# A transformer block on one core: first MLP cut into blocks of 464 tokens instead of 384, with fewer resident weight slots

## The chip, the cores and the metric

The kernel runs on one core of a Trainium2 chip. Its engines work side by side, each through its own list of instructions: TensorE (PE) multiplies matrices, VectorE (DVE), ScalarE (ACT) and GpSimd (POOL) work element by element, and SyncE (SP) issues the DMAs. The metric is the device time of one launch in microseconds; three runs of the kernel before gave 1130.8, 1130.98 and 1131.02, with a median of 1130.98.

## The reference

```
scores = (q @ k^T) / 8 + bias(pos)            # 4 batches, 8 heads, 576 positions, 64 per head
attn   = softmax(scores) @ v                  # -> x: 2304 tokens x 512
h = x @ w_in;   g = h - tanh(h)               # first MLP:  512 -> 2048
x = g @ w_out                                 #             2048 -> 512
gate = sigmoid(x @ w_gate);  val = x @ w_val  # second MLP: 512 -> 1536, twice
out  = (gate * val) @ w_out2                  #             1536 -> 512
```

The bias is a small MLP of the relative position. All is fp32; the MLP weights come in as float64.

## The kernel before

There are three stages: bias and attention, the first MLP, the second MLP. Each fp32 operand of an MLP product is split into a high part that PE multiplies at full rate (`fp32r`) and the rest, and a product is three matmuls, high by high, low by high, high by low (`P3`, L694, L764).

**First MLP.** The 2304 tokens are cut into blocks of `TBS[1]` = 384 columns, six of them. A step `n` of `STEPS` takes one block and two of the sixteen slices of 128 hidden units. It goes through the engines as a pipeline: `first` (PE, 24 matmuls into one of two PSUM tiles, `even` and `odd`), `second` (ACT, squares and tanh), `third` (DVE, five operations on both slices at once, which replace h - tanh(h) by a polynomial where h is small), `fourth` (ACT and POOL, split into high and low), `fifth` (PE, 24 matmuls into four accumulators `acc`), and at the end of a half-block `sixth` (the accumulators go to `o` and by DMA to `x2s`). PE takes `first(n)` and then `fifth(n-2)`. Half of the hidden units are done for all blocks, then the other half, whose `sixth` adds (L780) to what the first half stored. PSUM's eight banks are full: twice two for `up`, four for `acc`.

**Weights.** `Weights` turns each float64 tile of 512 KB into fp32: `load` (DMA, two buffers `wraw`), `scan` (ACT), `make` (four DVE operations, L578 to L576), `split` (ACT high, POOL low). The first 32 items (`RES`) are the first MLP's; each keeps a slot of SBUF, 15 of them are made during the attention. The other 36 are the second MLP's: their tiles are stored in DRAM (`wsc`). `W.step` does one item at a step of the first MLP: in steps 2 to 47, but not in three of the last (`X0_STEPS`) nor where a `sixth` of the second half is due (four more steps), which makes 39. The rest is done in the second MLP by the generator `convert`, which is asked once in each product slot and has 7 stops for an item.

**Second MLP.** `PAIRS` lists 18 rounds, each with 128 times two hidden units of gate and value, over a third of the tokens. Seven products (a Strassen form, `PRODUCTS`) of six matmuls each are done for two halves (`m`), so a round has 14 product slots (`slot2`), with `down` (six 512-column matmuls, L922) in every odd one. A round reads nine weight tiles of 512 KB back from `wsc` (`feed`, L855), in strict order, into any slot that is free. There are 14 such slots: 12 of the first MLP's (`RING_SLOTS`) as its last block leaves them and two new ones.

The `tile` calls say what may be overwritten when; the order on each engine is the order of the code.

Of the kernel before, what the change touches and what calls it, by code (L numbers as in the profile page):

```python
# [19 lines left out]
NT = NB * S  # L20
# [7 lines left out]
def bias_phase(tc, pools, par, bsc, during):  # L28
# [9 lines left out]
    heat = yp.tile([128, 512], F32, name="heat", bufs=1)  # L38
    nc.gpsimd.memset(heat, 0.0)
    ph = spare.tile([128, 2, 512], F32, name="sc")  # L40
    for i in range(HEAT):
        T.matmul(ph[:, i % 2], heat[:, 0:128], heat, start=True, stop=True)
    scl = yp.tile([128, S // 4], F32, name="scl", bufs=1)
# [421 lines left out]
STEPS = [(1, b, f) for b in range(NT // TBS[1]) for f in range(HALF)]  # L465
STEPS += [(1, b, f) for b in range(NT // TBS[1]) for f in range(HALF, NF1 // NPR)]
# [7 lines left out]
X_SLOTS, T_SLOTS, RING_SLOTS = tuple(range(14)), (14, 15), 12  # L474
STAGE1 = (0, 1, 2, 3)
# [14 lines left out]
class Weights:  # L490


    def __init__(self, nc, wi, wo, wg, wv, wo2, stage, wsc):
        self.nc, self.stage, self.wsc = nc, stage, wsc
        col = lambda w, n, f, k0, nk: dram_ap(w.bitcast(I32), 256 * f + 256 * n * k0, [[2 * n, 128], [256 * n, nk], [1, 256]])
        row = lambda w, f: dram_ap(w.bitcast(I32), 128 * f * 2 * DM, [[2 * DM, 128], [1, 2 * DM]])
        self.of = {}
        use = [("i", f) for f in range(FA)] + [("o", f) for f in range(FA)]
        for f in range(FA, NF1):
            use += [("i", f), ("o", f)]  # L500
        self.items = []
# [12 lines left out]
        self.clock = self.lag = 0  # L514
        self.pending = []
# [73 lines left out]
    def split(self):  # L589
        i = self.done  # L590
        if i >= min(self.made, RES):
            return [], []
        self.done += 1
        w = self.out[i] = self.slot(i)
# [71 lines left out]
def mlps(tc, st, xr, x0, W, xs, x2s, y2s, out, consts):  # L666
# [5 lines left out]
    TB = TBS[1]  # L672
    xt, xraw = {}, {}

    def x_load(blk, kt):
        kind, b, half = blk
        m = xr.tile([128, TB], F32, name="xm")
        nc.sync.dma_start(m, xs[128 * kt:128 * kt + 128, TB * b:TB * b + TB])
        xraw[blk, kt] = m

    def x_split(blk, kt):
        m = xraw.pop((blk, kt))
        t = xh[BLOCKS.index(blk) % 2].tile([128, 2, TB], F32R, name="xt")
# [6 lines left out]
    def project(w, blk, p):  # L690
        for kt in range(4):
            x = xt[blk, kt]
            for i, (a, c) in enumerate(P3):
                T.matmul(p[:, 0:TB], w[:, a, 128 * kt:128 * kt + 128], x[:, c], start=(kt == 0 and i == 0), stop=(kt == 3 and i == 2))  # L694

    ph, s1, s2, ac, part = {}, {}, {}, {}, {}

    def first(n):
        kind, b, f = STEPS[n]
        p = (even, odd)[n % 2].tile([128, 2, 512], F32, name="up")  # L700
        ph[n] = p[:, :, 0:TB]
# [34 lines left out]
    def halves(x):  # L736
        h, l = (ps.tile([128, TB], F32R, name=y) for y in ("gh", "gl"))
# [14 lines left out]
    def fifth(n):  # L752
# [6 lines left out]
        for j in range(NPR):  # L759
            w = W.get("o", NPR * f + j)  # L760
            h, l = parts[j]
            for d in range(4):
                for i, (a, c) in enumerate(((0, h), (1, h), (0, l))):
                    T.matmul(ac[blk][d][:, 0:TB], w[:, a, 128 * d:128 * d + 128], c, start=(begin and j == 0 and i == 0),  # L764
                             stop=(end and j == NPR - 1 and i == 2))

    def partial(n):
        kind, b, f = STEPS[n]
        for d in range(4):
            o = ob.tile([128, DM], F32, name="o")  # L770
            nc.sync.dma_start(o[:, 0:TB], x2s[128 * d:128 * d + 128, TB * b:TB * b + TB])
            part[b, d] = o

    def sixth(n):
        kind, b, f = STEPS[n]
        blk = block(n)
        for d, p in enumerate(ac.pop(blk)):
            if blk[2] == 1:
                o = part.pop((b, d))
                V.tensor_add(o[:, 0:TB], p[:, 0:TB], o[:, 0:TB])  # L780
            else:
                o = ob.tile([128, DM], F32, name="o")
                (V.tensor_copy if d % 2 else A.copy)(o[:, 0:TB], p[:, 0:TB])  # L783
            W.later(lambda d=d, o=o: nc.sync.dma_start(x2s[128 * d:128 * d + 128, TB * b:TB * b + TB], o[:, 0:TB]))
# [25 lines left out]
    def src_load(tau, kt):  # L810
        sx[kt] = x0.tile([128, TP], F32, name="xt")
# [47 lines left out]
    freed = {W.of[k, f]: LAST[1, f // NPR] + (3 if k == "o" else 1) for k in "io" for f in range(FA, NF1)}  # L859
    RING = sorted(freed, key=lambda i: (freed[i], i))  # L860

    def convert():
        while W.made <= W.n:
            highs, lows, mixes, conv = W.step()
            for i, f in enumerate(conv[:2]):
                f()
                yield i == 0
# [8 lines left out]
            yield False  # L876
# [177 lines left out]
    for n in range(N1 + 3):  # L1054
        if n < N1:
            W.tick()
        if n == 2:
            acc = st.enter_context(tc.tile_pool(name="ps_a", bufs=4, space=PSUM, side="right"))
        acts = second(n - 1) if ok(n - 1) else []
# [3 lines left out]
        if 2 <= n < N1 and n not in X0_STEPS and not any(ends(m) and block(m)[2] for m in due(n - 1, 2)):  # L1063
# [15 lines left out]
        if n == N1:  # L1079
# [5 lines left out]
            W.open(st.enter_context(tc.tile_pool(name="wx", bufs=1)), RES, RES + 2)  # L1085
            free += [RES, RES + 1]
# [6 lines left out]
        for m in due(n - 1, 2):  # L1093
            if ends(m):
# [50 lines left out]
def tile_attention_then_two_mlps(ctx: ExitStack, tc: tile.TileContext, qT, kT, vP, par, wi, wo, wg, wv, wo2, ident, out, xs=None):  # L1145
# [8 lines left out]
    with tc.manual_schedule():  # L1154
# [49 lines left out]
        W.open(ctx.enter_context(tc.tile_pool(name="wb", bufs=1, side="right")), EARLY + MORE, RES)  # L1204
# [58 lines left out]
```

## Time and profile before

| | |
|---|---|
| median of three runs | 1130.98 us |
| profiled execution, its own time | 1131.97 us |
| its span | 1130.2 us |
| PE busy | 1113.5 us, 99% |
| DVE / ACT / POOL busy | 809.6 / 669.5 / 642.6 us |
| first MLP on PE | from 301.8 us to 719.4 us, mixed at both ends with its neighbours |

The profile is that of one execution; its own time is 1.0 us above the median of the timed runs, and 1.8 us of it lie outside the span. Busy times of PE are sums over matmuls whose ends are modelled and overlap, so the pace of PE is read from the starts of matmuls in the timeline, not from their durations.

### The profile page before, as it was taken

How to read it: one execution, taken by the hardware profiler on the slowest of the kernel's cores; microseconds unless marked ns; L12 is line 12 of the kernel's file. 1: busy time of each engine (PE TensorE's matmuls, PEld its weight loads, DVE VectorE, ACT ScalarE, POOL GpSimd, SP SyncE). 2: the span in 40 equal slices, each digit the busy share in tenths (PEclk: the TensorE clock that was granted, in tenths of full speed). 3: DMA queues.
4: the chain of work that ended last, by engine and by line, in shares of the span. 5: the costliest groups of instructions: out<-in, count | busy, mean ns of one | idle time of the engine just before them, and what ended most of it. 6: DMA issues, size and time to landing. Idle time of an engine off the chain costs nothing.

```text
span 1130.2 us, 20776 instructions
## 1 busy us (share of the span) xinstructions
PE 1113.5 (99%) x7324; PEld 982.6 (87%) x7324; DVE 809.6 (72%) x1444; ACT 669.5 (59%) x1320; POOL 642.6 (57%) x597
## 2 busy tenths in 40 slices
PE   8999999999999999999999999999999999999998
PEld 3466677777789999999999999999999999999997
DVE  8988888888589988898888888556566444434423
ACT  8987787887667767677667667235354332423221
POOL 0046767767555645596858666465486574524532
PEclk9999999999999999999999999999999999999999
DMA  7845455463223323366564665987987898667671
GB/s 255 287 151 174 139 163 165 144 193 112 83 76 105 124 85 109 120 205 201 204 214 159 229 200 215 345 323 273 341 329 283 321 380 306 238 238 268 234 271 57
DMA packets 107783, 235.14 MB, mean 208 GB/s; under 512 B 12704, under 2 KB 53152, under 8 KB 107680
## 3 DMA queue, kind: packets, MB, share of 16 engines
q1 hardware_dynamic: 107536, 233.69, 59.7%
q8 instruction: 58, 0.95, 0.3%
q14 instruction: 45, 0.37, 0.1%
q10 hardware_dynamic: 144, 0.13, 0.0%
HBM read 172.55 MB, written 61.22 MB: 207 GB/s over the span
## 4 chain that ended last, share of the span: by engine, by line
PE 88%; DVE 4%; POOL 2%; ACT 2%; issue 2%; DMA 2%; DVEq 0%; SPq 0%; POOLq 0%; ACTq 0%
PE sum L906 23%; PE acc L764 16%; PE up L694 16%; PE acc L922 9%; PE sc L243 6%; PE pt L285 5%; PE pv L343 5%; PE up L922 4%; DVE y L68 2%; PE pv L340 2%; PE bt L82 1%; DMA wsc<-w 1%; POOL n L275 1%; DVE n L257 1%; PE pf L290 1%
## 5 line engine op out<-in xcount | busy, mean ns | idle before, releaser
L906 PE MATMUL sum<-w,w 128*128 128x384 f32 x1512 | 279.8, 335 | 0.2 <-ACT e L970 0.2
L906 PEld LDWEIGHTS sum<-w,w 128*128 128x128 f32 x1512 | 265.5, 188 | 10.0 <-ACT e L970 0.6
L694 PE MATMUL up<-xt,w 128*128 128x384 f32 x1152 | 208.4, 335 | 0.3 <-DVE t L734 0.3
L694 PEld LDWEIGHTS up<-xt,w 128*128 128x128 f32 x1152 | 200.1, 188 | 2.2 <-issue 1.6
L764 PE MATMUL acc<-gh,w 128*128 128x384 f32 x768 | 195.4, 335 | 0.6 <-DVE o L780 0.5
L275 POOL TENSOR_SCALAR n<-n,rec 128x576 f32<-128x576 f32 x144 | 108.4, 766 | 131.6 <-DVE rec L271 128.8
L745 POOL TENSOR_TENSOR gl<-t,gh 128x384 fp32r<-128x384 f32 x96 | 103.8, 1102 | 89.3 <-issue 53.9
L585 POOL TENSOR_TENSOR w<-wu,w 128x512 fp32r<-128x512 f32 x86 | 125.9, 1476 | 25.0 <-ACT w L587 25.0
L764 PEld LDWEIGHTS acc<-gh,w 128*128 128x128 f32 x768 | 138.2, 188 | 1.9 <-DVE o L783 1.1
L962 POOL TENSOR_TENSOR gl<-e,gh 128x384 fp32r<-128x384 f32 x54 | 59.1, 1096 | 121.8 <-ACT gh L738 121.7
L764 PE MATMUL acc<-gl,w 128*128 128x384 f32 x384 | 128.3, 334 | 0.0
L257 DVE CUSTOM_DVE_ANT_0 n<-sc,bias 128x576 f32<-128x576 f32 x144 | 103.9, 755 | 20.9 <-PE sc L243 18.9
L264 ACT ACTIVATE n<-n,mn 128x576 f32<-128x576 f32 x144 | 111.8, 787 | 0.3 <-DVE mn L257 0.3
L725 ACT ACTIVATE z<-z,c 128x768 f32<-128x768 f32 x48 | 45.1, 941 | 77.0 <-DVE up L722 77.0
L922 PE MATMUL acc<-w,gh 128*128 128x512 f32 x288 | 89.5, 392 | 0.0
L738 ACT CAST gh<-t 128x384 fp32r<-128x384 f32 x114 | 57.7, 515 | 53.0 <-POOL t L998 51.5
L730 DVE TENSOR_TENSOR t<-up,t 128x768 f32<-128x768 f32 x48 | 45.9, 957 | 54.0 <-ACT t L711 53.4
L987 DVE TENSOR_TENSOR e<-sum,e 128x384 f32<-128x384 f32 x70 | 38.9, 556 | 62.8 <-PE sum L906 62.1
L285 PE MATMUL pt<-ident,n 128*128 128x128 f32 x576 | 80.1, 279 | 1.7 <-POOL n L275 1.2
L685 POOL TENSOR_TENSOR xt<-xm,xt 128x384 fp32r<-128x384 f32 x48 | 49.3, 1048 | 48.6 <-ACT xt L684 47.1
L285 PEld LDWEIGHTS pt<-ident,n 128*128 128x128 f32 x576 | 62.6, 140 | 13.4 <-issue 8.6
L343 PE MATMUL pv<-at,vs 128*64 128x320 f32 (+1 forms) x512 | 73.2, 409 | 0.0
(115 smaller groups left out, 2125.3 us busy)
## 6 DMA issues: line engine op xcount, KB each, us to landing
w<-wsc SPq DMA_DIRECT2D x162, 512.0 KB, 6.1
wsc<-w SPq DMA_DIRECT2D x54, 512.0 KB, 5.7
wraw<-in_wo SPq DMA_DIRECT2D x28, 512.0 KB, 4.2
xm<-xs SPq DMA_DIRECT2D x48, 192.0 KB, 3.2
x2s<-o SPq DMA_DIRECT2D x48, 192.0 KB, 3.9
wraw<-in_wi SPq DMA_DIRECT2D x16, 512.0 KB, 4.1
xt<-x2s SPq DMA_DIRECT2D x20, 384.0 KB, 8.0
wraw<-in_wg SPq DMA_DIRECT2D x24, 256.0 KB, 3.4
```

The lines of the kernel that those rows point to most:

```text
L243: T.matmul(sc[u, t][:, hf, 0:288], q[r, 128 * s:128 * s + 128], k[r, o:o + 288], start=(i == 0), stop=(i == 2))
L257: V.tensor_tensor_reduce(n.rearrange("p (a b) -> p a b", a=2), s[:, :, 0:288], bias[t].rearrange("p (a b) -> p a b", a=2), -0.125, 3.0e38, ...
L264: A.activation(n, n, AF.Exp, bias=m, scale=-1.0, accum_out=nsum[u, t // 4][:, t % 4:t % 4 + 1])
L275: G.tensor_scalar(n, n, nrec[u, t // 4][:, t % 4:t % 4 + 1], 1.0, ALU.mult, ALU.mult)
L285: T.transpose(pt[:, i], n[:, o:o + 128], ident)
L343: T.matmul(p[0][64 * a:64 * a + 64, 0:N], v[:, c - 1, a], main[:, c - 1, a * N:a * N + N], start=False, stop=(c == 4))
L585: self.nc.gpsimd.tensor_sub(w[:, 1], x, w[:, 0].bitcast(F32))
L694: T.matmul(p[:, 0:TB], w[:, a, 128 * kt:128 * kt + 128], x[:, c], start=(kt == 0 and i == 0), stop=(kt == 3 and i == 2))
L745: G.tensor_sub(l, x[:, j], h.bitcast(F32))
L764: T.matmul(ac[blk][d][:, 0:TB], w[:, a, 128 * d:128 * d + 128], c, start=(begin and j == 0 and i == 0), stop=(end and j == NPR - 1 and i = ...
L906: T.matmul(p, w[:, a, o:o + 128], x[:, c], start=(fresh and kp == 0 and i == 0), stop=(kp == 1 and i == 2), skip_group_check=True)
L922: T.matmul(sums[3 * t + d], x[:, c], w[:, a], start=(begin and i == 0), stop=(end and i == 2))
```

## The change

The first MLP's blocks are 464 tokens wide, with 448 in the last, so there are five; its tiles are allocated 512 columns wide (`TA`), and every use takes the columns that the block has. To make room, the 32 items of the first MLP share 28 slots: the items 28 to 31 go into the slots 0 to 3 (`HOME`) once the first half no longer needs these, and the order of the items is changed so that these are `w_in` tiles. In the second MLP 8 slots of the first MLP and 4 new ones take the reloads, 12 in all. `sixth` of the second half is moved to the front of its step, DVE does the five operations of `third` straight after it, and the step now converts a weight item as others do. `W.step` starts at step 3. `convert` has 5 stops for an item instead of 7, and a raw load is issued one slot after its buffer is free instead of two. In the bias stage two small tiles share memory with others.

```diff
-TBS = (None, 384, 384)
+TBS = (None, 512, 384)
+BW1 = 464
+BLK = [(BW1 * b, min(BW1, NT - BW1 * b)) for b in range(-(-NT // BW1))]
-RES = 32
+RES, NSLOT = 32, 28
+HOME = {28: 0, 29: 1, 30: 2, 31: 3}
-X_SLOTS, T_SLOTS, RING_SLOTS = tuple(range(14)), (14, 15), 12
-STAGE1 = (0, 1, 2, 3)
+X_SLOTS, T_SLOTS, RING_SLOTS, MORE2 = (10, 11, 12, 13, 4, 5, 6, 7, 8, 9, 0, 1, 2, 3), (14, 15), 8, 4
+STAGE1 = (6, 7, 8, 9)
...
-                T.matmul(p[:, 0:TB], w[:, a, 128 * kt:128 * kt + 128], x[:, c], start=(kt == 0 and i == 0), stop=(kt == 3 and i == 2))
+                T.matmul(p[:, 0:x.shape[-1]], w[:, a, 128 * kt:128 * kt + 128], x[:, c], start=(kt == 0 and i == 0), stop=(kt == 3 and i == 2))
...
-            self.later(self.load, 2)
+            self.later(self.load, 1)
...
             for i, f in enumerate(conv[:2]):
                 f()
-                yield i == 0
+                if i == 0:
+                    yield True
...
             for f in mixes:
                 f()
-            yield False
             W.scan()
             yield True
...
+        sums_in = [m for m in due(n - 1, 2) if ends(m) and block(m)[2]]
+        for m in sums_in:
+            sixth(m)
...
-        if 2 <= n < N1 and n not in X0_STEPS and not any(ends(m) and block(m)[2] for m in due(n - 1, 2)):
+        if 3 <= n < N1 and n not in X0_STEPS:
...
+        if sums_in:
+            zip_run(vecs)
+            vecs = []
         zip_run(vecs, conv)
...
-            W.open(st.enter_context(tc.tile_pool(name="wx", bufs=1)), RES, RES + 2)
-            free += [RES, RES + 1]
+            W.open(st.enter_context(tc.tile_pool(name="wx", bufs=1)), NSLOT, NSLOT + MORE2)
+            free += range(NSLOT, NSLOT + MORE2)
```

**PE, in the second half of the first MLP.** Before, a step's 24 matmuls of `first` and the start of `fifth`:

```order
L694 MATMUL up<-xt,w_2388 128x384 x12
L694 MATMUL up<-xt,w_2629 128x384 x12
L764 MATMUL acc<-gh,w_3355 128x384 x2
L764 MATMUL acc<-gl,w_3355 128x384
L764 MATMUL acc<-gh,w_3355 128x384 x2
```

And of the change:

```order
L699 MATMUL up<-xt,w_5585 128x464 x12
L699 MATMUL up<-xt,w_5777 128x464 x12
L769 MATMUL acc<-gh,w_6133 128x464 x2
L769 MATMUL acc<-gl,w_6133 128x464
L769 MATMUL acc<-gh,w_6133 128x464 x2
```

The pattern of a step is the same; a matmul has 464 columns instead of 384, and there are 40 such steps instead of 48, so 1920 matmuls (1536 of 464 columns and 384 of 448) instead of 2304.

**DVE, where a half-block of the second half ends** (`o<-acc,o` is `sixth`, the rows on `up` and `t` are `third`, those on `wu` are `make`). Before:

```order
L734 COPY_PREDICATED t<-z,up 128x768
L730 TENSOR_TENSOR t<-up,t 128x768
L731 SCALAR_TENSOR_TENSOR up<-z,up 128x2x384
L722 SCALAR_TENSOR_TENSOR up<-z,up 128x2x384
L733 SCALAR_TENSOR_TENSOR up<-q,up 128x2x384
L734 COPY_PREDICATED t<-z,up 128x768
L780 TENSOR_TENSOR o<-acc,o 128x384 x4
L730 TENSOR_TENSOR t<-up,t 128x768
L578 TENSOR_SCALAR wu<-wu 128x512
```

And of the change:

```order
L739 COPY_PREDICATED t<-z,up 128x2x464
L787 TENSOR_TENSOR o<-acc,o 128x464 x4
L735 TENSOR_TENSOR t<-up,t 128x2x464
L736 SCALAR_TENSOR_TENSOR up<-z,up 128x2x464
L727 SCALAR_TENSOR_TENSOR up<-z,up 128x2x464
L738 SCALAR_TENSOR_TENSOR up<-q,up 128x2x464
L739 COPY_PREDICATED t<-z,up 128x2x464
L582 TENSOR_SCALAR wu<-wu 128x512
L583 TENSOR_SCALAR wu<-wu 128x512
L584 SCALAR_TENSOR_TENSOR wu<-wraw,wu 128x512
L580 SCALAR_TENSOR_TENSOR wu<-wraw,wu 128x512
```

The four additions stand ahead of the step's five operations instead of behind them, and a weight item follows where there was none.

**SP, at the passage to the second MLP** (`w<-wsc` is a reload; the number after `wsc` is the tile's place in its round). Before:

```order
L784 DMA x2s<-o 128x384 x4
L855 DMA w_9146<-wsc_4_69 128x1024
L855 DMA w_9148<-wsc_5_70 128x1024
L855 DMA w_9150<-wsc_6_71 128x1024
L855 DMA w_9152<-wsc_7_72 128x1024
L855 DMA w_9197<-wsc_8_73 128x1024
L855 DMA w_9199<-wsc_0_74 128x1024
L771 DMA o<-x2s 128x384 x4
L855 DMA w_9251<-wsc_1_75 128x1024
L855 DMA w_9253<-wsc_2_76 128x1024
L855 DMA w_9255<-wsc_3_77 128x1024
L855 DMA w_9257<-wsc_4_78 128x1024
```

And of the change:

```order
L791 DMA x2s<-o 128x464 x4
L862 DMA w_8442<-wsc_4_69 128x1024
L862 DMA w_8444<-wsc_5_70 128x1024
L862 DMA w_8489<-wsc_6_71 128x1024
L862 DMA w_8491<-wsc_7_72 128x1024
L862 DMA w_8493<-wsc_8_73 128x1024
L862 DMA w_8495<-wsc_0_74 128x1024
L777 DMA o<-x2s 128x448 x4
L862 DMA w_8547<-wsc_1_75 128x1024
L862 DMA w_8549<-wsc_2_76 128x1024
```

The first loads are the same, but they end two tiles earlier: the place 2 of the second round instead of the place 4, because there are 12 slots instead of 14.

## Rows read from the trace of the kernel before

**Rows 1.** The page, part 1: busy time of the engines over the span.
```profile
PE 1113.5 (99%) x7324; PEld 982.6 (87%) x7324; DVE 809.6 (72%) x1444; ACT 669.5 (59%) x1320; POOL 642.6 (57%) x597
```

**Rows 2.** Stretches: PE, PEld, DVE, ACT, POOL busy; PEclk, DMA share, GB/s.
```profile
320.00:704.00 384.00, 383.13 (x2204) 381.54 (x2203) 336.49 (x429) 267.50 (x434) 252.59 (x209) 1.00 0.49 164
...
735.00:960.00 225.00, 225.00 (x1180) 209.53 (x1179) 123.04 (x199) 84.18 (x169) 135.60 (x116) 1.00 0.86 319
```

**Rows 3.** Timeline of PE in the first MLP: start, length, line, count.
```profile
669.97 4.32 PE L694 MATMUL up<-xt,w 128*128 128x384 f32 x24
674.13 0.51 PE L764 MATMUL acc<-gh,w 128*128 128x384 f32 x2
...
686.61 4.32 PE L694 MATMUL up<-xt,w 128*128 128x384 f32 x24
691.45 0.59 PE L764 MATMUL acc<-gh,w 128*128 128x384 f32 x2 [0.52 <-DVE o L780]
```

**Rows 4.** Timeline of PE in the kernel's last microseconds, 512 columns alone.
```profile
1120.01 0.61 PE L922 MATMUL acc<-w,gh 128*128 128x512 f32 x2
...
1124.77 0.61 PE L922 MATMUL acc<-w,gh 128*128 128x512 f32 x2
```

**Rows 5.** Timeline of PE in the second MLP, 384 and 512 columns by turns.
```profile
799.84 2.24 PE L906 MATMUL sum<-w,w 128*128 128x384 f32 x12
801.92 0.63 PE L922 MATMUL acc<-w,gh 128*128 128x512 f32 x2
...
803.31 2.25 PE L906 MATMUL sum<-w,w 128*128 128x384 f32 x12
```

**Rows 6.** Timeline of PE at the start of the first MLP.
```profile
299.97 0.66 PE L285 MATMUL pt<-ident,n 128*128 128x128 f32 x4
301.31 0.63 PE L285 MATMUL pt<-ident,n 128*128 128x128 f32 x4 [0.69 <-POOL n L275]
...
327.19 0.34 PE L764 MATMUL acc<-gl,w 128*128 128x384 f32 x1
327.81 4.46 PE L694 MATMUL up<-xt,w 128*128 128x384 f32 x24 [0.27 <-DVE t L734]
```

**Rows 7.** Timeline of POOL there.
```profile
294.95 1.99 POOL L685 TENSOR_TENSOR xt<-xm,xt 128x384 fp32r<-128x384 f32 x2
296.91 4.35 POOL L275 TENSOR_SCALAR n<-n,rec 128x576 f32<-128x576 f32 x6
```

**Rows 8.** Groups by line: count, busy, mean ns, idle before.
```profile
L722 DVE SCALAR_TENSOR_TENSOR up<-z,up 128x768 f32<-128x768 f32 x48 | 45.6, 951 | 0.2
L734 DVE COPY_PREDICATED t<-z,up 128x768 f32<-128x768 int32 x48 | 50.8, 1058 | 0.8
L578 DVE TENSOR_SCALAR wu<-wu 128x512 f32<-128x512 f32 x68 | 62.6, 921 | 0.3
L576 DVE SCALAR_TENSOR_TENSOR wu<-wraw,wu 128x512 int32<-128x512 int32 x68 | 56.7, 834 | 0.1
L579 DVE TENSOR_SCALAR wu<-wu 128x512 int32<-128x512 int32 x68 | 32.4, 476 | 0.0
L780 DVE TENSOR_TENSOR o<-acc,o 128x384 f32<-128x384 f32 x24 | 11.8, 551 | 2.0 <-PE acc L764 2.0
L939 DVE TENSOR_TENSOR o<-acc,o 128x512 f32<-128x512 f32 x7 | 4.8, 685 | 0.0
L685 POOL TENSOR_TENSOR xt<-xm,xt 128x384 fp32r<-128x384 f32 x48 | 49.3, 1048 | 48.6 <-ACT xt L684 47.1 <-DMA xm<-xs 1.3
L585 POOL TENSOR_TENSOR w<-wu,w 128x512 fp32r<-128x512 f32 x86 | 125.9, 1476 | 25.0 <-ACT w L587 25.0
```

**Rows 9.** DMA from 735 to 960 us: rate in 40 slices, the queue.
```profile
GB/s 295 208 330 381 386 226 387 405 202 155 397 415 371 224 294 396 272 169 396 413 145 162 290 405 410 410 385 411 326 99 312 400 402 414 350 373 409 124 240 379
...
q1 hardware_dynamic: 24014, 71.60, 85.4%
```

**Rows 10.** The reload's line L855: landing over the whole kernel.
```profile
DMA to landing us min/median/max: 3.1/6.1/10.3
```

More of the change, by code (lines that the diff above doesn't have):

```diff
@@ L37, in bias_phase @@
     w1c, b1c, wb, ps = pr[:, 0:1], pr[:, 1:2], pr[:, 4:36], pr[:, 36:36 + S // 4]
-    heat = yp.tile([128, 512], F32, name="heat", bufs=1)
+    heat = yp.tile([128, S], F32, name="y")
     nc.gpsimd.memset(heat, 0.0)
@@ L41, in bias_phase @@
     for i in range(HEAT):
-        T.matmul(ph[:, i % 2], heat[:, 0:128], heat, start=True, stop=True)
-    scl = yp.tile([128, S // 4], F32, name="scl", bufs=1)
+        T.matmul(ph[:, i % 2], heat[:, 0:128], heat[:, 0:512], start=True, stop=True)
+    scl = ps
     V.tensor_scalar(scl, ps, w1c, None, ALU.mult)
@@ L464 @@
 HALF = FA // NPR
-STEPS = [(1, b, f) for b in range(NT // TBS[1]) for f in range(HALF)]
-STEPS += [(1, b, f) for b in range(NT // TBS[1]) for f in range(HALF, NF1 // NPR)]
+STEPS = [(1, b, f) for b in range(len(BLK)) for f in range(HALF)]
+STEPS += [(1, b, f) for b in range(len(BLK)) for f in range(HALF, NF1 // NPR)]
 LAST = {(k, f): n for n, (k, b, f) in enumerate(STEPS)}
@@ L498, in __init__ @@
         use = [("i", f) for f in range(FA)] + [("o", f) for f in range(FA)]
-        for f in range(FA, NF1):
+        for f in range(FA, FA + 4):
             use += [("i", f), ("o", f)]
+        use += [("o", f) for f in range(FA + 4, NF1)] + [("i", f) for f in (14, 15, 12, 13)]
         self.items = []
@@ L593, in split @@
         self.done += 1
-        w = self.out[i] = self.slot(i)
+        w = self.out[i] = self.slot(HOME.get(i, i))
         def low():
@@ L671, in mlps @@
     nq, nz, warm = consts
-    TB = TBS[1]
+    TA, TB = TBS[1:]
     xt, xraw = {}, {}
@@ L676, in x_load @@
         kind, b, half = blk
-        m = xr.tile([128, TB], F32, name="xm")
-        nc.sync.dma_start(m, xs[128 * kt:128 * kt + 128, TB * b:TB * b + TB])
+        c0, w = BLK[b]
+        m = xr.tile([128, TA], F32, name="xm")[:, 0:w]
+        nc.sync.dma_start(m, xs[128 * kt:128 * kt + 128, c0:c0 + w])
         xraw[blk, kt] = m
@@ L682, in x_split @@
         m = xraw.pop((blk, kt))
-        t = xh[BLOCKS.index(blk) % 2].tile([128, 2, TB], F32R, name="xt")
+        t = xh[BLOCKS.index(blk) % 2].tile([128, 2, TA], F32R, name="xt")[:, :, 0:BLK[blk[1]][1]]
         A.copy(t[:, 0], m)
@@ L708, in second @@
         p = ph[n]
-        t, z, q = (k.tile([128, 2, TB], F32, name=x) for k, x in ((pk, "t"), (pm, "z"), (pq, "q")))
+        t, z, q = (k.tile([128, 2, BW1 if k is pq else TA], F32, name=x)[:, :, 0:BLK[STEPS[n][1]][1]] for k, x in ((pk, "t"), (pm, "z"), (pq, "q")))
         s1[n] = t, q, z
@@ L736, in halves @@
     def halves(x):
-        h, l = (ps.tile([128, TB], F32R, name=y) for y in ("gh", "gl"))
+        h, l = (ps.tile([128, TA], F32R, name=y)[:, 0:x.shape[-1]] for y in ("gh", "gl"))
         A.copy(h, x)
@@ L763, in fifth @@
                 for i, (a, c) in enumerate(((0, h), (1, h), (0, l))):
-                    T.matmul(ac[blk][d][:, 0:TB], w[:, a, 128 * d:128 * d + 128], c, start=(begin and j == 0 and i == 0),
+                    T.matmul(ac[blk][d][:, 0:BLK[b][1]], w[:, a, 128 * d:128 * d + 128], c, start=(begin and j == 0 and i == 0),
                              stop=(end and j == NPR - 1 and i == 2))
@@ L776, in sixth @@
         blk = block(n)
+        c0, w = BLK[b]
         for d, p in enumerate(ac.pop(blk)):
@@ L810, in src_load @@
     def src_load(tau, kt):
-        sx[kt] = x0.tile([128, TP], F32, name="xt")
+        sx[kt] = x0.tile([128, 2 * TA], F32, name="xt")[:, 0:TP]
         nc.sync.dma_start(sx[kt], x2s[128 * kt:128 * kt + 128, TP * tau:TP * tau + TP])
@@ L857, in feed @@
             issued[0] += 1
-    freed = {W.of[k, f]: LAST[1, f // NPR] + (3 if k == "o" else 1) for k in "io" for f in range(FA, NF1)}
+    freed = {HOME.get(W.of[k, f], W.of[k, f]): LAST[1, f // NPR] + (3 if k == "o" else 1) for k in "io" for f in range(FA, NF1)}
+    freed = {i: n for i, n in freed.items() if i >= 2 * FA}
     RING = sorted(freed, key=lambda i: (freed[i], i))
@@ L1093, in mlps @@
         for m in due(n - 1, 2):
-            if ends(m):
+            if ends(m) and m not in sums_in:
                 sixth(m)
@@ L1129, in mlps @@
         p, j = PAIRS[s // SLOTS2][3], s % SLOTS2
-        if s > SLOTS2 // 2 and not crowded and not (heavy and p == 0 and j > SLOTS2 - 3):
+        if s > SLOTS2 // 2 and not crowded and not (heavy and (s % 2 if s < SLOTS2 else p == 0 and j > SLOTS2 - 3)):
             heavy = next(conv, False)
```

17 lines of the change are left out of this document (9 added, 8 removed).

## The prediction

> **What bounds the kernel now.** I read the shares of busy time first: PE is busy for 1113.5 of 1130.2 us, and no other engine above 72% [rows 1]. So a microsecond is won or lost only where PE's stream of matmuls gets shorter or where PE stands still. The stretches say the same stage by stage: PE has 383.13 of 384 us in the first MLP and all of 225 us in the second while it converts weights [rows 2]. The second number to see there is the clock, granted in full (1.00, which is 2.4 GHz) in both; and the third DVE's 336.49 us, 88%, the nearest engine behind PE in the first MLP.
>
> Busy is not yet pace, so I went to PE's timeline and took the starts. 24 matmuls of 384 columns go from 669.97 to 674.13 [rows 3], 173.3 ns each. 384 columns at 2.4 GHz, one a cycle, are 160 ns; so each matmul costs 13.3 ns on top. Is that a cost of the matmul or of its columns? The kernel's last microseconds hold 512 columns alone: from 1120.01 to 1124.77 there are seven times three, 4.76 us or 226.7 ns each [rows 4], which is 213.3 + 13.3. The same remainder at both widths: a fixed cost per matmul, in a stream of one width. Where the widths take turns it is not so good: twelve of 384 take 2.08 us as ever, but six of 512 take from 801.92 to 803.31, 231.7 ns each, 18.3 ns above their columns [rows 5].
>
> **The change part by part.**
>
> *The stream of the first MLP.* Tokens times passes stay, the matmuls go from 2304 to 1920. Before: 2304 x 173.3 ns = 399.3 us. Behind: 464 columns are 193.3 + 13.3 = 206.7 ns, 448 are 200.0 ns, so 1536 x 206.7 + 384 x 200.0 = 317.4 + 76.8 = 394.2 us. That is 384 x 13.3 ns less, **-5.1 us**, all of it on the path, since PE hardly waits here. Bounds: the reading of 4.76 us is good to 0.01 us, half a nanosecond a matmul, which gives about 1 us either way; and if 464 columns paid the 18.3 ns of the mixed rows, it would be 1536 x 211.7 + 384 x 205.0 = 403.9 us, 4.6 us more than before. I take the fixed 13.3 ns, because a block is a stream of one width and both rows of such streams agree.
>
> The Trainium skill ("TensorE: Matmul & The Clock Gate", section on the back-to-back issue gap) speaks against this: it puts the gap of isolated matmuls at full clock to the columns at 2.4 GHz plus about 2.5 ns. By that figure the sum would lose only 384 x 2.5 ns, an estimate of 1.0 us; the 13.3 ns of these rows do not agree with it.
>
> *Engines beside PE.* A step now takes 48 x 206.7 ns = 9.92 us, before 8.32. DVE's five operations of `third` are four of 951 ns and one of 1058, 4.86 us, and a weight item is 921 + 476 + 2 x 834 ns = 3.07 us [rows 8]: 7.93 of 8.32 us where both fall. The addition's rows (551 ns at 384 columns, 685 at 512) give 1.05 ns a column, so 160 columns more add 0.17 us to each of the five: 5.70 + 3.07 = 8.77 of 9.92. DVE gains room. POOL's difference costs 1048 ns at 384 and 1476 at 512 columns [rows 8], 3.3 ns a column, +0.27 us at 464; it stays at two thirds. Cost: nothing, covered by PE's stream; if that cover were gone, DVE would be next.
>
> *Where a half-block ends.* At 686.61 PE begins 24 matmuls, which end 4.16 us later at 690.77; the next begins at 691.45 because DVE's additions came late [rows 3]: 0.68 us, of one block end. With the additions ahead of `third` they are done 4 x 0.64 = 2.5 us into the step, and PE wants the accumulators only 4.96 us into it; this wait goes. What it delays: the five operations behind it end 2.5 + 5.7 = 8.2 us into the step, where PE wants that PSUM tile at 9.92; the weight item that was left out before follows, to 11.3 us, and then the next `third` with its item ends at 11.3 + 8.8 = 20.1 where PE wants its tile at 19.84. So up to 0.3 us can appear at each of three ends (the last two have no item). One more wait, the first refill of a PSUM tile (327.19 to 327.81, 0.62 us where 0.17 is the pace [rows 6]), shrinks: PE covers 48 x 33 ns = 1.6 us more, the chain of two ACT and five DVE operations grows by about 1.2. I take -0.7 and -0.3 for the two: **-1.0 us**, bounds -1.1 and +1.0.
>
> *The start.* At 301.31 PE had waited 0.69 us for POOL's normalisation, and POOL had done two `xt` differences right before those [rows 6, 7]. They get 0.27 us longer each: **+0.5 us**, bounds 0 and +1.1 (two more such pairs).
>
> *Weights of the first MLP.* One item a step from step 3; item 31 is split at step 20 and wanted at step 22. A whole step, 9.9 us, lies between, so it is hidden; if it were not, PE would stand once for some microseconds.
>
> *The second MLP.* Its matmuls are the same. Two things get tighter. The items done before it are those of steps 3 to 36, 34 instead of 39, and the five left over are fitted in by 5 stops instead of 7: about 20 items in the time of 15. An item moves 0.52 MB in and, on average, 1.5 tiles of 0.52 MB out, so 6.6 MB join the 71.6 MB from 735 to 960 us, and the queue's share goes from 85.4% to 93%; the fullest slices show about 415 GB/s, the mean would be 348 [rows 9]. And with 12 slots instead of 14, a reload in the middle of a round is issued 8 product slots before its use instead of 10. Two slots take 803.31 - 799.84 = 3.47 us [rows 5], so 13.9 us ahead instead of 17.3; reloads land in 6.1 us, at most 10.3 [rows 10]. That still fits, with 3.6 us to spare for SP's own waits in its strict order. Behind a late reload stand all later ones in that queue, and PE. I take **+0.5 us**, bounds 0 and +10 (below).
>
> *The rest.* Two tiles that share memory at the start, another order of slots: nothing, each beside engines that wait anyway.
>
> Sum: -5.1 - 1.0 + 0.5 + 0.5 = -5.1 us. The profiled execution took 1131.97 us, so it would be 1126.9; the timed median lies 1.0 us lower, which gives **1125.9 us**. The forecast's own range, with 1 us on the pace and the bounds of the waits but not of the reloads, is 1123.5 to 1128.5.
>
> **The rivals.**
>
> *A. The 13.3 ns belong to the columns, not to the matmul.* Then 173.3 ns become 173.3 x 464/384 and the first MLP keeps its 399.3 us; with the waits' sum of 0, the time is 1131.0. For it: PE's weight loads, 87% busy [rows 1], and an overhead at 464 columns that no row shows. Against it: 226.7 ns at 512, where it would be 231.1. The mixed rows with 231.7 fit it, as long as one takes them for the rule. If only a small part of the 13.3 ns is the matmul's own, the time lies between this and the forecast, near here. With the 2.5 ns of the Trainium skill's section on the back-to-back issue gap it would be 1130.0, the same verdict; I give that 0.03 of A's chance.
>
> *B. The reloads starve PE (slower).* One place: tiles 1 to 3 of a round from 735 to 960 us, issued 8 slots ahead. It decides from the point where issue to landing, with SP's wait ahead of it, exceeds 13.9 us. At 93% of a queue whose slowest landing is 10.3 us already, half as much again is 15.5 us, 1.6 us too late, in each of the nine rounds of that stretch: 14 us, of which the next rounds' earlier issue gives some back; I put 10 us, 1136. For it: slices at 410 GB/s stand next to each other in the middle of the stretch [rows 9]. Against it: PE stood for nothing in these 225 us, though the queue was at that rate for 20 us on end.
>
> *C. 464 columns pay what 512 pay in the mixture*, 18.3 ns: +4.6 instead of -5.1, so 1135.6. For it: most 512-column matmuls of this kernel do. Against it: the stream of 512 alone [rows 4].
>
> **How the numbers follow.** A run of this kernel can tell about 0.2%, 2.3 us, from no change, so faster means below 1128.7, slower above 1133.2. The forecast gets 0.75, A 0.13, B 0.08, C 0.04. All of the forecast's own range counts as faster, A as the same, B and C as slower: 0.75, 0.13, 0.12. To hold 8 in 10 the range goes from 1123.0 past the forecast's upper end to A, 1131.5; B and C are left out.
>
> **What would show it.** In the profile after: 1920 matmuls in the first MLP, 24 of 464 columns 4.96 us apart from start to start (5.08 for C, 5.03 for A); PE's count down by 384; no wait of PE for additions into `o`, and a wait for `copy_predicated` of 0.3 us at most behind them; PE without idle time from 735 to 960 us, with the DMA share above 0.9 and reloads landing within 13 us. The prediction is wrong if the spacing at 464 columns is above 209 ns, or if PE waits for `w<-wsc` for more than 2 us in all.

## The result and the profile after

Four runs of the changed kernel took 1135.93 to 1137.40 us, median 1136.74, beside 1130.89 for four of the kernel before: a ratio of 1.0052, interval 1.0034 to 1.0069. It is slower by about 5.9 us where 5.1 us less were forecast, and outside the range. The profiled execution took 1135.93 us, with a span of 1134.1, 3.9 us above that of before.

First the page of the kernel after, part 1, and the three stretches (the third is the passage between the two MLPs). They answer to [rows 1, 2].

```profile
PE 1114.4 (98%) x6940; PEld 944.9 (83%) x6940; DVE 823.7 (73%) x1398; ACT 661.0 (58%) x1262; POOL 638.2 (56%) x573
```

```profile
320.00:704.00 384.00, 383.50 (x1845) 346.00 (x1845) 326.78 (x365) 254.26 (x369) 227.71 (x176) 1.00 0.43 144
735.00:960.00 225.00, 220.65 (x1143) 204.33 (x1142) 145.27 (x214) 89.42 (x177) 149.73 (x121) 0.99 0.90 334
704.00:735.00 31.00, 30.70 (x164) 28.77 (x163) 16.38 (x27) 8.69 (x18) 16.12 (x14) 1.00 0.96 361
```

PE issues 384 matmuls fewer, as the change says, and is nevertheless busy for 0.9 us more. In the first MLP it stands still for nothing worth naming, before and after. In the second it was busy all of 225 us; now 4.35 us are missing and the clock's mean is 0.99. So there are two questions: why 384 matmuls fewer gave nothing, and where PE stood.

The pace, from PE's timeline of the kernel after in the first MLP (start, length, line, count), beside [rows 3]:

```profile
564.38 0.58 PE L769 MATMUL acc<-gh,w 128*128 128x464 f32 x2
...
569.40 5.18 PE L699 MATMUL up<-xt,w 128*128 128x464 f32 x24
574.41 0.58 PE L769 MATMUL acc<-gh,w 128*128 128x464 f32 x2
```

24 matmuls take 5.02 and 5.01 us from start to start, 209 ns each; 4.96 us had been forecast, 5.03 was the mark of rival A. Over all of them the mean is 208.95 ns at 464 columns and 204.61 at 448, so the first MLP's matmuls take 1536 x 208.95 + 384 x 204.61 = 399.5 us. Before, by the same count, it was 2304 x 173.47 = 399.7.

The second place is the eighth round of the second MLP. PE's timeline of the kernel after:

```profile
878.49 2.25 PE L914 MATMUL sum<-w,w 128*128 128x384 f32 x12
880.58 0.63 PE L930 MATMUL acc<-w,gh 128*128 128x512 f32 x2
...
881.97 1.21 PE L914 MATMUL sum<-w,w 128*128 128x384 f32 x6
886.11 2.24 PE L914 MATMUL sum<-w,w 128*128 128x384 f32 x6 [2.93 <-DVE e L987]
888.14 1.05 PE L930 MATMUL acc<-w,gh 128*128 128x512 f32 x2
```

PE stands for 2.93 us, and then six matmuls take 2.03 us where twelve took 2.09 ahead of the wait. The stretches of those microseconds (the last three numbers are PE's clock, the DMA share and GB/s) say why:

```profile
882.00:886.10 4.10, 1.18 (x7) 0.85 (x5) 0.94 (x3) 1.70 (x4) 0.05 (x1) 1.00 1.06 401
886.20:889.40 3.20, 3.20 (x9) 2.94 (x10) 2.90 (x5) 1.30 (x3) 3.20 (x3) 0.50 1.02 410
889.60:892.60 3.00, 3.00 (x18) 2.87 (x17) 0.83 (x3) 0.52 (x1) 2.52 (x3) 1.00 1.02 403
```

Behind the wait the granted clock is 0.50, which is 1.2 GHz, for some 3.4 us; at half the pace that costs another 1.7 us. That round took 27.7 us from its first `sum` to the next round's; an undisturbed one takes 22.9.

What PE waited for is found by asking each releaser what released it. DVE L987, the evacuation of a bank, is one of many behind a weight operation. The same microseconds of DVE, ACT and SP in the kernel after:

```profile
867.46 1.23 DVE L580 SCALAR_TENSOR_TENSOR wu<-wraw,wu 128x512 int32<-128x512 int32 x1
...
879.83 0.56 DVE L981 TENSOR_TENSOR e<-sum,e 128x384 f32<-128x384 f32 x1 [1.87 <-PE sum L914]
885.16 0.43 DVE L582 TENSOR_SCALAR wu<-wu 128x512 f32<-128x512 f32 x1 [4.77 <-ACT wu L568]
885.50 0.55 DVE L987 TENSOR_TENSOR e<-sum,e 128x384 f32<-128x384 f32 x1
```

```profile
877.30 0.48 ACT L978 COPY e<-sum 128x384 f32<-128x384 f32 x1 [1.44 <-PE sum L914]
884.40 0.66 ACT L568 ACTIVATE wu<-wraw 128x512 f32<-128x512 f32 x1 [6.62 <-DMA wraw<-in_wv]
```

```profile
868.86 0.32 SPq L862 DMA_DIRECT2D w<-wsc  x1
870.12 0.32 SPq L952 DMA_DIRECT2D y2s<-o  x1
870.80 0.32 SPq L862 DMA_DIRECT2D w<-wsc  x1
872.02 1.00 SPq L644 DMA_DIRECT2D wsc<-w  x2
873.97 0.38 SPq L551 DMA_DIRECT2D wraw<-in_wg  x1
875.19 0.38 SPq L551 DMA_DIRECT2D wraw<-in_wv  x1
```

Read it from the bottom. SP issued the raw float64 tile (L551) at 873.97 and 875.19, though DVE had read the old one out of that buffer with its L580 that ended at 868.7. In between stood, in SP's strict order, two reloads, a store of `o` and the two stores of converted weights (L644). They went out slowly, because the queue was full: in the trace each of these issues, the raw load's too, begins within 0.1 us after the landing of the DMA that SP had issued eight before it (the reload of 866.01 landed at 873.91, the raw load went out at 873.97). The tile landed 9.1 us after its second issue; ACT waited 6.62 us for it, DVE 4.77 for ACT with the evacuation queued behind, and PE for the evacuation.

The other wait is the one that had been feared, for a reload, in the fifth round:

```profile
804.44 0.40 PE L930 MATMUL acc<-w,gl 128*128 128x512 f32 x1
806.19 2.15 PE L914 MATMUL sum<-w,w 128*128 128x384 f32 x11 [1.35 <-DMA w<-wsc]
```

This reload had been issued at 797.65, behind two stores of converted weights (795.14 and 796.40), only 7.2 us before PE wanted it, and it landed at 806.05, 8.4 us after its issue.

The account by stages, in us from the span's start, from the starts of PE's rows:

| | before | after | difference |
|---|---|---|---|
| first `up` of the first MLP | 301.80 | 301.01 | -0.8 |
| first `sum` of round 1 | 727.0 | 724.7 | -2.3 |
| of round 5 | 819.3 | 818.8 | -0.5 |
| of round 7 | 865.1 | 864.6 | -0.5 |
| of round 8 | 888.0 | 892.3 | +4.3 |
| end of the span | 1130.20 | 1134.14 | +3.9 |

(Rounds count from 0 here, so the eighth round is 7.) From the first `up` to round 1 the change gained 1.5 us, the fifth round lost 1.5 (1.8 from round 1 to round 5), the eighth 4.8.

### The profile page after: what moved, and what is told of

It reads as the page before. It is cut to its first block, busy times and chain, and to the rows that moved or that the text cites. A ratio compares the mean times of both kernels' runs of the same rounds, so it can differ in the third digit from the quotient of the medians.

```text
span 1134.1 us, 19782 instructions
## 1 busy us (share of the span) xinstructions
PE 1114.4 (98%) x6940; PEld 944.9 (83%) x6940; DVE 823.7 (73%) x1398; ACT 661.0 (58%) x1262; POOL 638.2 (56%) x573
## 4 chain that ended last, share of the span: by engine, by line
PE 88%; DVE 5%; DMA 3%; ACT 1%; issue 1%; POOL 1%; DVEq 0%; SPq 0%; ACTq 0%; POOLq 0%
PE sum L914 21%; PE up L699 17%; PE acc L769 17%; PE acc L930 8%; PE sc L243 6%; PE pt L285 6%; PE pv L343 5%; PE up L930 4%; DMA w<-wsc 2%; PE bt L82 2%; PE pv L340 2%; DVE y L68 1%; DVE n L257 1%; DMA wraw<-in_wv 1%; POOL n L275 1%
## 5 line engine op out<-in xcount | busy, mean ns | idle before, releaser
L699 PE MATMUL up<-xt,w 128*128 128x464 f32 (+1 forms) x960 | 207.2, 371 | 0.5 <-DVE t L739 0.5
L699 PEld LDWEIGHTS up<-xt,w 128*128 128x128 f32 x960 | 179.8, 188 | 21.7 <-issue 1.6
L769 PE MATMUL acc<-gh,w 128*128 128x464 f32 (+1 forms) x640 | 185.0, 370 | 0.0
L750 POOL TENSOR_TENSOR gl<-t,gh 128x464 fp32r<-128x464 f32 (+1 forms) x80 | 100.5, 1278 | 101.9 <-PE acc L769 55.7
L769 PEld LDWEIGHTS acc<-gh,w 128*128 128x128 f32 x640 | 120.2, 188 | 13.1
L769 PE MATMUL acc<-gl,w 128*128 128x464 f32 (+1 forms) x320 | 118.7, 371 | 0.0
L730 ACT ACTIVATE z<-z,c 128x928 f32<-128x928 f32 (+1 forms) x40 | 42.7, 1068 | 95.4 <-DVE up L727 95.3
L743 ACT CAST gh<-t 128x464 fp32r<-128x464 f32 (+2 forms) x98 | 53.8, 566 | 57.5 <-POOL t L1006 55.2
L735 DVE TENSOR_TENSOR t<-up,t 128x928 f32<-128x928 f32 (+1 forms) x40 | 44.6, 1115 | 53.1 <-ACT t L716 53.0
L690 POOL TENSOR_TENSOR xt<-xm,xt 128x464 fp32r<-128x464 f32 (+1 forms) x40 | 47.2, 1202 | 55.0 <-ACT xt L689 55.0
```

Of the source, the lines that this page charges most:

```text
L699: T.matmul(p[:, 0:x.shape[-1]], w[:, a, 128 * kt:128 * kt + 128], x[:, c], start=(kt == 0 and i == 0), stop=(kt == 3 and i == 2))
L750: G.tensor_sub(l, x[:, j], h.bitcast(F32))
L769: T.matmul(ac[blk][d][:, 0:BLK[b][1]], w[:, a, 128 * d:128 * d + 128], c, start=(begin and j == 0 and i == 0), stop=(end and j == NPR - 1 ...
```

## Experiments

**The pace by width.** A kernel that computes nothing of the reference: streams of 48 `fp32r` matmuls of one width, each behind a pause, three times over with pauses of different length; then streams without a pause, twelve of 384 by turns with six of 512, and at the end some streams with work for the other engines and the DMAs written beside them.

```diff
+WIDTHS = (384, 400, 416, 432, 448, 464, 480, 496, 512)
+        for rep in range(3):
+            for width in WIDTHS:
+                stall(acc[0], rep + 1)
+                many(width, acc)          # 48 matmuls, four accumulators by turns
```

> Streams of 48 fp32r matmuls each, a new 128x128 weight for every matmul, three to an accumulator, at 384 to 512 columns in steps of 16; three passes with a pause of one, two or three small DVE copies ahead of each stream, then streams that follow each other without a pause, 12 of 384 and 6 of 512 by turns, and five widths beside busy DVE, ACT, POOL and DMA. Nothing of the reference is computed; the output only fills the shape. Theory 1 (the price is the TensorE's own, by width): the quiet streams give again what the two kernels show, 173.3 ns at 384, 202.6 to 206.7 at 448, 208.9 to 210 at 464, and 226.7 or 231.6 at 512, and other widths lie off columns/2.4 GHz + 13.3 ns by 0 to 7 ns. Rival 2 (other engines or DMA slow the wide matmuls of the real kernel): quiet streams give 200.0 at 448 and 206.7 at 464, and only those beside busy engines are dearer. Rival 3 (a matter of phase, set when a stream starts): the same width has different spacings in the three passes.

PE's timeline in it, three of the streams (a tiny matmul, which waits for the stream, stands between them):

```profile
23.79 8.59 PE L45 MATMUL acc<-x,w 128*128 128x384 f32 x48
32.22 0.19 PE L52 MATMUL tiny<-s 128*64 128x64 f32 x1
...
69.50 10.31 PE L45 MATMUL acc<-x,w 128*128 128x464 f32 x48
79.64 0.19 PE L52 MATMUL tiny<-s 128*64 128x64 f32 x1
...
101.02 11.15 PE L45 MATMUL acc<-x,w 128*128 128x512 f32 x48
112.00 0.19 PE L52 MATMUL tiny<-s 128*64 128x64 f32 x1
```

From 384 to 512 columns a stream grows from 8.43 to 10.98 us, 53.1 ns a matmul; the 128 columns are 53.3 ns at 2.4 GHz. That is the fixed overhead of the prediction, and between 384 and 464 it does not hold. The mean of the 12th to the 31st spacing of each stream of the first pass (the first spacing is 255 to 315 ns, a few behind it are uneven), and what it has above its columns and 13.3 ns:

| columns | 384 | 400 | 416 | 432 | 448 | 464 | 480 | 496 | 512 |
|---|---|---|---|---|---|---|---|---|---|
| ns | 173.3 | 180.0 | 188.3 | 195.9 | 202.7 | 210.0 | 216.7 | 223.3 | 226.7 |
| above | 0 | 0 | 1.7 | 2.5 | 2.7 | 3.3 | 3.3 | 3.3 | 0 |

The table is the same in all three passes to 0.1 ns. The work for the other engines depended on nothing and so ran ahead of its place: it stands beside the first pass, where POOL was busy for 0.96 of the stream of 464 columns and the DMAs moved 316 GB/s, while nothing but DVE's pauses stands beside the third; 464 columns took 210.0 ns in both. At the end, where it was meant to be, DVE alone was busy, for 0.23 to 0.51 of a stream, with the same paces. Where a stream followed another without a pause, 464 columns took 208.9 ns behind 448 columns, as in the changed kernel, and 210.0 behind 512. So the price is TensorE's own and goes with the width; neither POOL, DVE nor the DMAs make it. In the mixture, 512 columns took 230.6 to 230.8 ns and 384 took 173.7, about what the second MLP shows [rows 5].

**What of the second MLP's changes costs.** Three versions of the kernel before: with five stops for a weight item and the raw load one slot earlier; with 12 slots for the reloads instead of 14; with both.

```diff
-            self.later(self.load, 2)
+            self.later(self.load, 1)
-                yield i == 0
+                if i == 0:
+                    yield True
-            yield False
```

```diff
-            free += [RES, RES + 1]
+            free += []
```

> The kernel before with the change's convert alone: 5 stops for a weight item instead of 7, raw loads one slot after their buffer is free. Fifteen items are left for the second MLP, as before, not twenty. Theory 1 (a raw load that lands late stops ACT, and behind it DVE and PE, once an item comes every 5 slots): ACT waits for wraw by several us between 735 and 960 us and PE stands for 1 to 5 us, 1132 to 1136. Rival 2 (the 12 reload slots alone do it): no PE idle time in that stretch, 1131.0 within 0.5.

> The kernel before with 12 reload slots in the second MLP instead of 14 (the two new ones are not used), 7 stops. Theory 1: reloads come 3.5 us later against their use, the least slack of a reload falls from 4.8 to about 1.3 us, PE does not wait, 1131.0 within 0.5. Rival 2 (the ring is what starves PE): PE waits for w<-wsc in several rounds, 2 to 5 us in all, 1133 to 1136.

> The kernel before with both, 5 stops and 12 slots. Theory 1: little more than with 5 stops alone, 0 to 1.5 us from reloads that are now late as well, 1132 to 1137. Rival 2: the same as with 12 slots alone. If only the two together cost something, it is the DMA queue's total that counts, and this run alone is 3 us or more above 1131.

Measured, ratios to the same 25 runs of the kernel before (1131.42 us): five stops 1131.95 us, 1.0008 (0.9998 to 1.0017); 12 slots 1130.54, 0.9992 (0.9983 to 1.0002); both 1134.02, 1.0026 (1.0017 to 1.0035). Each alone is covered, the two together are not. PE's timeline with both:

```profile
800.37 1.21 PE L906 MATMUL sum<-w,w 128*128 128x384 f32 x6
802.96 1.28 PE L906 MATMUL sum<-w,w 128*128 128x384 f32 x6 [1.38 <-DMA w<-wsc]
```

It is a wait for a reload in the same round as in the changed kernel, at another place of it, with 384-column blocks in the first MLP; it is 1.4 of the 2.6 us. The wait at 883 is not there: ACT's longest wait for a raw tile is 2.0 us with both, 1.4 in the kernel before.

**The stores' place in SP's order.** The changed kernel, with the stores of converted weights issued six product slots behind their turn instead of four. Besides, four stores of `x2s` at the passage to the second MLP go out behind two reloads instead of ahead of them; nothing else moves in SP's order, and no byte fewer is read or written.

```diff
-            W.lag = 4
+            W.lag = 6
```

> The changed kernel with the stores of converted weights issued 6 product slots after they are asked for instead of 4 (the lag of the second MLP). Theory 1 (the raw load comes late because SP stands in its strict order behind a store whose tile POOL has not made yet): SP no longer waits there, ACT's wait for wraw falls from 7 us to under 2, PE's stall at 883 us goes, 1132 to 1134. Rival 2 (the load is late because the DMA engines are full): the wait stays within 1 us of what it was, 1136 to 1138.

1130.37 us, 0.9993 of the kernel before (0.9984 to 1.0002): 6.4 us less than the changed kernel. SP's timeline in the eighth round, and the stretch from 735 to 960 us:

```profile
871.54 0.38 SPq L551 DMA_DIRECT2D wraw<-in_wg  x1
872.60 0.38 SPq L551 DMA_DIRECT2D wraw<-in_wv  x1
873.85 1.61 SPq L644 DMA_DIRECT2D wsc<-w  x2
```

```profile
735.00:960.00 225.00, 224.71 (x1173) 208.19 (x1172) 147.77 (x217) 90.20 (x179) 155.12 (x125) 1.00 0.92 345
```

The raw tile now goes ahead of the stores, 2.4 and 2.6 us earlier. Of that 1.0 us is PE itself, which is earlier here by that much because the reload's wait in the fifth round fell from 1.35 to 0.29 us. The tile lands 7.7 us after its second issue instead of 9.1, and PE is back at 224.71 of 225 us at full clock. The time is below the expected 1132 to 1134 us, since both waits shrank. The expectation's reason, a store whose tile POOL has not made yet, is not what the trace shows: SP waited for landings. The stretch of 20 us around the wait, in the changed kernel and with six slots:

```profile
866.00:886.00 20.00, 17.18 (x89) 15.54 (x88) 9.46 (x15) 6.48 (x14) 10.23 (x8) 1.00 1.04 406
```

```profile
865.00:885.00 20.00, 20.00 (x103) 18.05 (x102) 11.43 (x19) 8.15 (x16) 12.99 (x10) 1.00 1.04 405
```

The queue is full in both, and it was full in the kernel before as well (405 GB/s from 866 to 886 us). So the load of the queue is not what tells them apart; the order of issue decides which transfer is late while it is full. ACT's waits for raw tiles in that stretch, after and then with six slots (us in total, times, longest):

```profile
ACT wu L568 <- DMA wraw<-in_wv: 7.1, 2, 6.6
```

```profile
ACT wu L568 <- DMA wraw<-in_wv: 12.5, 6, 3.6
```

ACT's longest wait fell to 3.6 us, not to under 2 as expected. The sum grew and the time fell: here PE felt the longest single wait and not their sum, and the six shorter ones passed beside its work.

**Blocks of 512 and 384.** The changed kernel with the widths that pay no extra (and one buffer fewer in the attention, to make room), in three forms: alone; with a sixth stop for the items 50 to 61; with the stores six slots behind.

```diff
-BW1 = 464
-BLK = [(BW1 * b, min(BW1, NT - BW1 * b)) for b in range(-(-NT // BW1))]
+BW1 = 512
+WID = (512, 512, 512, 384, 384)
+BLK = [(sum(WID[:b]), w) for b, w in enumerate(WID)]
```

```diff
+            if 50 <= W.made < 62:
+                yield False
             W.scan()
```

> The changed kernel with blocks of 512, 512, 512, 384 and 384 tokens instead of 464 (four) and 448, still 1920 matmuls in the first MLP (one buffer less for the attention's output, to make room). Theory 1 (the price is TensorE's own and goes by width, as in the quiet streams: 226.7 ns at 512, 173.3 at 384): 1152 x 226.7 + 768 x 173.3 = 394.2 us for the first MLP's matmuls instead of 399.5, 5 us less, so 1131 to 1133 with the waits of the second MLP as they are. Rival 2 (beside busy engines 512 columns cost the 231.6 ns of the second MLP): 5.6 us more than that, no gain, 1136 to 1138.

> The kernel with blocks of 512 and 384 and, besides, 6 stops for the first twelve weight items of the second MLP and 5 for the rest (with 6 for all, the last round's tiles would not be there in time). Theory 1 (the stalls of the second MLP come from items that follow each other too fast for the DMA queue): PE's idle time from 735 to 960 us falls from 4.4 us and its slow clock after it goes, 1126 to 1130. Rival 2 (the stalls come from the 12 slots or the five more items, whatever the pace): as e5_512 within 1 us.

> The kernel after with blocks of 512, 512, 512, 384 and 384 tokens (as in e5_512) and with the stores of the converted weights issued six slots after their turn instead of four (as in e6_lag6). If the two causes are independent of each other, the parts add: e6_lag6 stood at 1130.4 us; the 512 and 384 columns give back 4.4 us of the matmuls' pace, and the wait of e5_512 near 664 us takes 2.3 us and the half clock behind it some 1.5, and its start 0.5: 1130.3 us, no wait of PE over 1 us in the second MLP. Rival: the second MLP is reached earlier or later and its wait comes back in whole (it depends on where the raw loads stand among the stores): 1135 to 1137 us.

Alone: 1135.82 us, 1.0043 (1.0026 to 1.006). The pace came as the table has it: 1152 matmuls at 227.13 ns and 768 at 173.72 are 395.1 us, 4.4 less than in the changed kernel. But the time stayed, since a new wait took the gain. PE's timeline of it at the end of the third block's second half, and the stretch behind:

```profile
664.25 0.34 PE L770 MATMUL acc<-gl,w 128*128 128x384 f32 x1
666.73 6.00 PE L700 MATMUL up<-xt,w 128*128 128x384 f32 x24 [2.14 <-DVE t L740]
672.56 0.51 PE L770 MATMUL acc<-gh,w 128*128 128x384 f32 x2
```

```profile
666.90:671.00 4.10, 4.10 (x16) 4.10 (x16) 4.10 (x6) 2.85 (x6) 3.80 (x4) 0.58 0.85 322
```

DVE, busy in all of it, is late with `third`, and again the clock falls behind the wait: 24 matmuls take 5.83 us instead of 4.17, so the spot costs about 2.3 + 1.7 us.

The sixth stop for twelve items removed the wait near 883 and gave others: 1136.44 us, 1.0043 (1.0026 to 1.006), with four waits for reloads, 5.1 us in all, the one in the fifth round as before and three further on, from 920 to 973 us. PE's waits from 735 to 1000 us in it:

```profile
PE sum L917 <- DMA w<-wsc: 5.1, 4, 2.3
```

With the stores six slots behind: 1129.89 us, 0.9989 (0.9979 to 0.9998), with the wait at 664 still there (2.2 us). Against the changed kernel the widths alone give -0.9 us, the stores alone -6.4 and both -6.9, so the two causes add up as independent ones.

**The additions ahead of `third`, alone.** The kernel before with only this part of the change, the weight item in that step included.

```diff
+        sums_in = [m for m in due(n - 1, 2) if ends(m) and block(m)[2]]
+        for m in sums_in:
+            sixth(m)
...
+        if sums_in:
+            zip_run(vecs)
+            vecs = []
```

> The kernel before with one part of the change: the additions at the end of a half-block stand ahead of the step's five DVE operations, and a weight item is converted there too (four more before the second MLP). Theory 1: the 0.68 us wait at 691 us goes and no new one of more than 0.3 us comes, 0.5 to 1.2 us faster, 1129.8 to 1130.9 beside its own run of before. Rival 2: DVE is late at the three ends with an item and PE waits 1 us at each, 1131.5 to 1134.

1136.91 us, 1.0053 (1.0038 to 1.0068). PE's waits in it from 320 to 735 us:

```profile
PE up L694 <- DVE t L734: 4.6, 5, 1.5
PE acc L764 <- POOL gl L745: 0.3, 1, 0.3
```

It is slower than either theory had it. The first of the five waits (0.28 us at 327 us) is that of the kernel before; the other four are new, 4.3 us in all. With steps of 384 columns DVE has 8.32 us for the additions, `third` and a weight item, and PE waits for it. With steps of 464 columns the same code shows one wait of 0.5 us.

**The 384-column blocks first.** The wait at 664 stands where the additions of a 512-token block fall into a 384-column step. If that is its cause, another order of the blocks removes it.

```diff
-WID = (512, 512, 512, 384, 384)
+WID = (384, 384, 512, 512, 512)
...
-            W.lag = 4
+            W.lag = 6
```

> As f1_512_lag6, but the blocks stand as 384, 384, 512, 512, 512. Theory of the wait near 664 us (the additions of a 512-token block on VectorE fall into a step of 384 columns, which is 8.3 us long instead of 10.9): in this order only the additions of a 384-token block fall into such a short step, once, as in e8_sixth, where it cost 1.1 to 1.7 us; the long wait and the half clock behind it go, so 1126.5 to 1128 us, faster than the kernel before by 3 us or more. Rival: the wait belongs to the change of width as such or to the place in the program (24 steps in): then it stays at 2 us or more, with the half clock, and the time at 1130 us. Rival: the second MLP's wait comes back: 1133 us or more.

1127.97 us, 0.9971 (0.9961 to 0.9981): the fastest version here, 3.1 us below the kernel before and 8.8 below the changed one. Its page, and PE's waits from 320 to 735 us:

```profile
PE 1110.8 (99%) x6940; PEld 932.8 (83%) x6940; DVE 825.8 (73%) x1398; ACT 659.8 (59%) x1262; POOL 638.8 (57%) x573
```

```profile
PE acc L770 <- DVE o L791: 0.6, 2, 0.4
PE sum L915 <- DVE e L996: 0.3, 1, 0.3
PE up L700 <- DVE t L740: 0.2, 1, 0.2
```

The long wait and the low clock behind it are gone. The gain over the other order, 1.9 us, is less than the 2.3 + 1.7 us of that spot; the short waits that came, 0.85 us in the first MLP, are a part of the rest, and the remainder is not traced. The rival that the wait belongs to the change of width or to that place in the program falls: this order changes width too.

## Why the prediction was wrong

**The stream, -5.1 us: this step failed.** It took the fixed 13.3 ns to hold at 464 and 448 columns "because a block is a stream of one width and both rows of such streams agree". Both rows were right, and the micro kernel shows the same 13.3 ns at 384, 400 and 512. Between them it is up to 3.3 ns more, and the trace of before had no row there. The term measured -0.2 us. Of the missing 4.9 us, 1536 x (208.95 - 206.7) is 3.5 and 384 x (204.61 - 200.0) is 1.8, less 0.4 us for what 173.47 is above 173.3. A's number for the stream came true and its reason did not: 512 columns alone have no 231 ns. C's is wrong too, in a stream of one width. The 1 us allowed for the pace was the error of reading two points; the error that counted was the line drawn between them.

**Block ends, -1.0 us: right.** Summed over PE's spacings in the first MLP that are over 60 ns longer than the pace, 2.6 us above the pace became 1.3, so -1.3. The additions' wait of [rows 3] and the first refill's of [rows 6] are gone, and the 0.3 us that "can appear at each of three ends" appeared once, as 0.50 us for `third`. The additions alone, in the kernel before, show what the wider step covered. PE's timeline of the kernel after at that one place:

```profile
659.43 0.37 PE L769 MATMUL acc<-gl,w 128*128 128x464 f32 x1
660.30 1.06 PE L699 MATMUL up<-xt,w 128*128 128x448 f32 x4 [0.50 <-DVE t L739]
```

**The start, +0.5 us: not to be told.** POOL's two differences take 2.32 us instead of 1.99 [rows 7], 0.33 us more where 0.54 had been reckoned, but the first `up` is 0.8 us earlier; over the versions run here it lies between 301.01 and 302.91, whatever the start's code, so its scatter hides the term.

**The second MLP, +0.5 us: this term was mis-sized.** It measured +6.2 from round 1 on (409.4 us to the end instead of 403.2). The sum of the queue's bytes was nearly right: 78.2 MB were expected from 735 to 960 us instead of 71.60, and it was 75.01 with PE's waits, which push work out of the stretch, and 77.31 with the stores six slots behind, where PE hardly waits. The failed reading is that the mean load of the queue was the question. While the queue is full, two deadlines in SP's order decided. For a reload, 1.35 us late, the forecast weighed the five stops and the 12 slots together, and they had to come together, but it left 3.6 us for SP's own waits: the late one was issued 7.2 us ahead of its use, where 13.9 us had been reckoned for the middle of a round. For the raw tile it had no term: that SP's stores stand ahead of it had not been looked at, nor that DVE evacuates PE's banks behind a weight operation. The third part, the low clock behind a long wait, no row of before could show, since PE never stood that long there.

**Rival B** had the sign and the time (1136), but for the reloads of nine rounds; they cost one wait of 1.35 us. The greater one came by a path that it does not name, so that its time came true is luck. Of the two marks neither tells clearly: the spacing at 464 columns is 209.2 and 208.75 ns in the two streams shown and 208.95 in the mean, beside a mark of 209, and PE waited for reloads for 1.4 us, under the 2 us named, while the time was lost to a wait of another name.

Left open: what in TensorE makes 416 to 496 columns dearer, and why of all rounds the fifth alone is late for a reload; the stores ahead of it have a part in it, since with them two slots later the wait is 0.29 us.

## What to carry to other kernels

Before a tile is made wider, measure the pace at that very width; two points that agree say nothing of the widths between. When slack is taken from several places at once, follow each in-order queue to the nearest deadline and look at the longest single wait, since here two waits with one of 6.6 us cost more than six of at most 3.6. A gain in one stage is measured best with the other stages' new waits taken out first; here other block widths and a later place for the stores together turned +0.5% into -0.3%.

## What the runs showed of the hardware

- A stream of `fp32r` matmuls at 2.4 GHz costs its columns and 13.3 ns at 384, 400 and 512 columns, but 1.7 to 3.3 ns more from 416 to 496; 512 columns (226.7 ns) cost only 3.4 ns more than 496. The Trainium skill ("TensorE: Matmul & The Clock Gate", section "Back-to-back issue gap") gives for isolated matmuls the columns at 2.4 GHz and about 2.5 ns; by that figure 464 columns would be 195.8 ns, an estimate, and the runs have 208.9 to 210.0.
- In the changed kernel 448 columns took 202.6 ns in the first half of the hidden units and 206.7 in the second, behind a short wait, and the kernel of widths has 464 columns at 208.9 and at 210.0 ns: the same width can settle at two paces.
- After a wait of 2.9 us PE's granted clock was 0.50 (1.2 GHz) for 3.4 us, and after the 2.14 us of the version with 512-token blocks it was 0.58 in the mean of 4.1 us. After a wait of 2.35 us at 962 us, in the version with the sixth stop, it stayed at 1.00. So the length of the wait alone does not tell whether the clock falls.
- The queue moved 405 to 406 GB/s for 20 us around 875 us in the kernel before, in the changed kernel and in the one with the stores six slots behind; PE stood for 2.93 us in the changed kernel alone, which issues in another order.
- From 735 to 960 us, 17 of SP's 152 issues in the kernel before and 41 of 163 in the changed kernel began within 0.15 us after the landing of the DMA that SP had issued eight before: there each issue waited for a landing.
